# Gating two row groups a step, early fetches tied to their own scatters, zeros kept in the rows' memory, and a new order of steps

## The chip, the cores and the metric

The kernel runs on one core of one Trainium2 chip. The metric is the device time of one execution in microseconds (us); lower is better. Every number below comes from the profile of the kernel before, from its timed runs, or from the two programs as they are built.

## What is computed

Eight sequences of 1856 rows of 256 values pass a spectral filter, and every filtered row then goes to one of 16 experts. Cut to what matters:

```python
X = np.fft.rfft(x, axis=1)                       # x: (8, 1856, 256)
Yr = Xr @ w_r - Xi @ w_i + b_r
Yi = Xr @ w_i + Xi @ w_r + b_i
Yr, Yi = soft_threshold(Yr, 0.01), soft_threshold(Yi, 0.01)
y = np.fft.irfft(Yr + 1j * Yi, n=1856, axis=1)   # 14848 rows of 256
g = argmax(y @ w_group)                          # 4 groups, gate = softmax value
e = argmax(y @ w_expert[g])                      # 4 experts a group, gate likewise
out = gate_g * gate_e * (relu(y @ w1[g, e]) @ w2[g, e])   # 256 -> 1024 -> 256
```

## The kernel before, in words

The sequences are taken in four pairs. For a pair TensorE runs the forward transform in two stages (`first_a`, L342, into `bank`; `f_mm`, L668, into `pg`), mixes real and imaginary parts with the weights (`m_part`, L723, into `pw`), and runs the inverse transform in two stages (`b_mm`, L771; `p_mm`, L790). Float32 operands are split into a rounded high part, cast on ScalarE, and a low rest, made on VectorE; so `xh` and `xl`, `wh` and `wl`. `m_both` (L723, step k) needs the high part of the sum of both parts, `s_high` (L703, step t, on ScalarE), and a bias that ScalarE writes into `pw` first (`m_bias`, L716, step j). `m_min` (L752 and L754, step o, VectorE) ends the mix; the last `o` of a pair opens its inverse transform (step r).

The rows that come out are turned (`p_turn`, L812), copied to `yt` (L816 on ScalarE, or VectorE), and multiplied with the gate weights (`g_mm`, L831, step G); VectorE turns the logits (`g_turn`, L841, step H), and the route steps (R, L210 to L280) choose the expert and the slot of each row. GpSimd then scatters the rows to the lists of their experts in DRAM, `xs_d` (L293, step S), 128 scatters in all, 32 for a pair, with two to four under way at a time. While the last pair is still routed, eight early jobs already work on the first 256-row pieces of four experts' lists: `e_fetch` (L472 and L477, step F, on SP's queue), `e_turn` (L481, T), `e_high` and `e_low` (L892, L896), `up_mm` (L907, U) and `down_mm` (L928, D). Behind all scatters come the remaining jobs (L520 onward), whose code is the same in both kernels.

Lists that are not full must hold zeros. `clear_steps` (step Z) writes them from a block of zeros with 17 transfers that ScalarE issues (L434 once, 130 KB; L436 sixteen times, 1170 KB each).

The order on TensorE, ScalarE, VectorE and SP is written out: a string `ORDER` of 1884 letters, one letter a step, is walked from the left, and each engine gets the instructions of its steps in that order. GpSimd's order is left to the scheduler. The loads and the first transform of pair 0 stand ahead of the string, in an order of their own; on SP they are the eight pieces of `x` for pair 0 (`big`), then weights, bias and tables, then four pieces of 1024 KB of pair 1's `x` into `v` (L355), then `CI` and `wg`.

Transfers of SP and of ScalarE share eight completion semaphores (`DMAHW0` to `DMAHW7` in the rows of order below), taken in turn in the order of the program. A transfer that takes one again is issued only when the transfer that had it before has landed; the engine that is to issue it waits in its own stream of instructions.

Of the kernel before, what the change touches and what calls it, by code (L numbers as in the profile page):

```python
# [10 lines left out]
F32 = mybir.dt.float32  # L11
# [10 lines left out]
K1 = 15  # L22
# [43 lines left out]
ejefgfhitgeukhijqeptukmoqfgmhicotupjmkfoqmoghepijtefguhkmimqootcjpukdqmfZgmoehiptojfZguemkhcqmoiotjpfZukgdqehi  # L66
mmoptojfZugcmmdkhqoeitopujkmfZgomqheitpclojufZgdmkehoqmitojpfZgukmmedqhplitfZgouojmmchocioktjeqpumfZgddokmqhci
otpjumedfZogmkqehitojpukmoqefZmogpjhitemmukofZogjhrqpitsumekmsfZrgohioqstjusepfZkqgmohripmfZssmotoeghriusjekts
mocjcqdupfZkdcqmgvdompcwlohjmifmtducexdgkohyqcivdopwGHlmcvemfjtoguwhiotkxquypjefkmdomgchvoiqtduGpjwxmkmfgqhyix
ltpoHGeoHjmumkoyfgoqhivtGpHRjeuwRRfkRmglqRxeomhioRpvtjfyRukmRRRqRgehmRRiptGRRomoRHfomujRvegRokhwRqxiRjtuwRpRfk  # L70
gRmxqRmhioopytjRuGmmyRHkqefoopgRhiemtjumGfkooRqgrhjiptuekRHfmegsRsmohiRrSqotussjpkmfmqvogowjpxheityukrqfGmgRom
phsHesmfoRitjouRgrkhieqstRmepsSmSoucRRjSSRvkwRdSRfcgSRxqRhmpyivdSocRtofgGuhRwcSmdljRRiHRdRRkqxomyecSStcRpRRoRd
dRufGljvghcwkHiRxmmqoRpeSytdojRRfScgRmvuhoRmwkqeiRtdlupojfGHSvRkqxmmwRRogpeyoShmSxiGtomvSufghjHRRkiqoteRRRSSRy
pjSuRkvRRmfqGoghwSpmioRteRjuRkRSSHfmxqoSpRghmRoyeRiRSwGtSmjvfwSSRRRRRuSgHkRqhiRxRtmoxRSoRpSyjeuRRkGRfqghimomyp
mmeoRHotoGHuRRfRjSghitrkujeqsRRspRmfkgomRqhrRopssmeSjRfiotRgumrhRitkSReqloRpSusRjfkesmgRRmoqhriotRSjRpuRmSskfW
# [98 lines left out]
def spectral_moe(ctx: ExitStack, tc: tile.TileContext, x, wri, bri, wgate, w1, w2, cst, out):  # L174
# [1219 lines left out]
```

## Time and profile before

| | |
|---|---|
| median of 3 runs | 1055.45 us (1054.57 to 1057.11) |
| the profiled execution | 1054.6 us, span 1052.8 us |
| mean granted TensorE clock | 0.993 |
| TensorE busy | 1016.0 us, 97% of the span |
| VectorE, ScalarE, GpSimd busy | 67%, 52%, 24% |

The profile shows one execution. An engine's row gives the start, the duration, the line, what is written and read, and in brackets how long the engine sat idle before it and which instruction or transfer ended that. A row may merge several instructions, with the count behind "x". The granted clock is 1.00 at 2.4 GHz and 0.50 at 1.2 GHz.

The stages can be read off lines: the first `f_mm` is at 17 us, the last `o` of the four pairs ends at 80.6, 161, 247.6 and 329.15 us, and the remaining jobs begin at 466.07 us.

### The profile page before, as it was taken

The page shows a single profiled execution, that of the slowest core. Times are in us where ns is not written, and L with a number is a line of the kernel's source. Part 1 is how long each engine was busy: PE and PEld are TensorE (multiplying, and loading weights), DVE is VectorE, ACT ScalarE, POOL GpSimd, SP SyncE. Part 2 cuts the span into 40 slices and gives each one's busy share as a digit, 9 for nine tenths or more (in the row PEclk, how much of TensorE's full clock was granted, in tenths as well). Part 3 has the DMA queues.
Part 4 walks back from the last instruction along what each step waited for, and adds up shares of the span by engine and source line. Part 5 has one row for each costly group of instructions (what it writes and reads, how often), then busy time and mean ns, then how long its engine had stood idle before and what let it go on. Part 6 is the DMA issues. An engine that isn't in the chain of part 4 may idle for free.

```text
span 1052.8 us, 20013 instructions
## 1 busy us (share of the span) xinstructions
PE 1016.0 (97%) x7078; PEld 857.9 (81%) x7078; DVE 704.4 (67%) x1764; ACT 549.6 (52%) x1428; POOL 255.1 (24%) x262
## 2 busy tenths in 40 slices
PE   7999999999996999999999999999999999999996
PEld 4886787677874678998899999988889899999995
DVE  6889678988987477647677656475465566566551
ACT  2664685575873464434554535455354455455442
POOL 1000003245355517641121211212211121212111
PEclk9999999999998999999999999999999999999998
DMA  9776401421132156565343232431431431432100
GB/s 379 289 308 239 162 1 38 158 87 69 51 103 81 65 140 185 171 204 148 113 138 112 59 109 53 145 115 49 136 111 51 138 107 52 146 113 63 33 26 25
DMA packets 110065, 125.62 MB, mean 119 GB/s; under 512 B 86250, under 2 KB 86923, under 8 KB 105098
## 3 DMA queue, kind: packets, MB, share of 16 engines
q1 hardware_dynamic: 91386, 74.31, 24.1%
q0 software_dynamic: 11888, 30.67, 7.8%
q10 hardware_dynamic: 6688, 19.34, 4.7%
q8 instruction: 57, 0.93, 0.4%
q14 instruction: 46, 0.38, 0.1%
HBM read 74.32 MB, written 51.75 MB: 120 GB/s over the span
## 4 chain that ended last, share of the span: by engine, by line
PE 79%; issue 6%; DVE 5%; DMA 4%; ACT 3%; POOL 2%; SPq 1%; POOLq 0%; ACTq 0%; DVEq 0%
PE ph L520 26%; PE py L592 16%; PE pw L723 11%; PE py L593 8%; PE pg L668 4%; PE ph L907 3%; DMA xs_d<-v,sloti 2%; PE bank L771 2%; PE bank L342 2%; PE bank L790 2%; PE bank L812 1%; PE py L611 1%; POOL xs_d L293 1%; PE pg L831 1%; PE pg L928 1%
## 5 line engine op out<-in xcount | busy, mean ns | idle before, releaser
L592 PE MATMUL py<-big,hh 128*128 128x512 f32 (+2 forms) x792 | 275.9, 393 | 0.1
L520 PE MATMUL ph<-xth,big 128*128 128x384 f32 (+14 forms) x1024 | 274.3, 346 | 1.6 <-DVE hl L528 0.8
L578 POOL DMA_INDIRECT out_dram<-yo,si x120 | 122.3, 1019 | 484.8 <-DVE si L315 234.0
L528 DVE SCALAR_TENSOR_TENSOR hl<-ph,hh 128x256 fp32r<-128x256 f32 x472 | 157.5, 372 | 98.4 <-ACT hh L524 71.6
L593 PE MATMUL py<-big,hl 128*128 128x256 f32 (+2 forms) x792 | 221.0, 279 | 0.0
L524 ACT ACTIVATE hh<-ph 128x256 fp32r<-128x256 f32 x472 | 140.2, 345 | 113.3 <-PE ph L520 112.6
L520 PEld LDWEIGHTS ph<-xth,big 128*128 128x128 f32 x1024 | 185.4, 188 | 13.6 <-ACT xth L506 1.9
L293 POOL DMA_INDIRECT xs_d<-v,sloti x128 | 126.2, 986 | 284.0 <-DVE big L754 147.8
L520 PE MATMUL ph<-xtl,big 128*128 128x384 f32 (+14 forms) x512 | 176.8, 345 | 1.2 <-DVE xtl L507 1.2
L592 PEld LDWEIGHTS py<-big,hh 128*128 128x128 f32 (+2 forms) x792 | 147.4, 186 | 34.6 <-issue 1.2
L593 PEld LDWEIGHTS py<-big,hl 128*128 128x128 f32 (+2 forms) x792 | 148.0, 187 | 0.3
L600 DVE SCALAR_TENSOR_TENSOR yo<-py,si,yo 128x256 f32<-128x256 f32 (+2 forms) x99 | 47.7, 482 | 108.9 <-ACT yo L599 108.9
L599 ACT ACTIVATE yo<-py,si 128x256 f32<-128x256 f32 (+2 forms) x99 | 46.8, 473 | 131.4 <-PE py L593 121.4
L520 PEld LDWEIGHTS ph<-xtl,big 128*128 128x128 f32 x512 | 96.3, 188 | 7.0 <-DVE xtl L507 2.3
L723 PE MATMUL pw<-wh,xh 128*128 128x256 f32 x360 | 81.3, 308 | 1.6 <-DVE pw L733 1.1
L745 ACT ACTIVATE th<-pw,CF 128x256 f32<-128x256 f32 x120 | 61.1, 526 | 36.8 <-PE pw L723 23.5
L723 PEld LDWEIGHTS pw<-wh,xh 128*128 128x128 f32 x360 | 54.3, 189 | 29.0 <-DVE pw L733 9.4
L723 PE MATMUL pw<-wh,xl 128*128 128x256 f32 x360 | 71.4, 280 | 0.9 <-DVE xl L707 0.9
L723 PE MATMUL pw<-wl,xh 128*128 128x256 f32 x360 | 71.0, 279 | 0.0
L668 PEld LDWEIGHTS pg<-CF,big 128*128 128x128 f32 x480 | 58.4, 191 | 12.6 <-issue 3.1
L668 PE MATMUL pg<-CF,big 128*128 128x128 f32 x480 | 64.6, 278 | 4.2 <-DVE xs L698 2.1
L723 PEld LDWEIGHTS pw<-wh,xl 128*128 128x128 f32 x360 | 54.9, 189 | 1.1 <-DVE xl L707 1.1
(187 smaller groups left out, 1557.4 us busy)
## 6 DMA issues: line engine op xcount, KB each, us to landing
xt<-in_w_dram SPq DMA_DIRECT2D x22, 1024.0 KB, 6.1
xs_d<-zero ACTq DMA_DIRECT2D x16, 1170.0 KB, 5.0
whole<-in_w_dram SPq DMA_DIRECT2D x16, 1024.0 KB, 8.1
xt<-in_x_dram SPq DMA_DIRECT2D x8, 1024.0 KB, 5.4
xg<-xs_d SPq DMA_DIRECT2D x48, 96.0 KB, 2.3
big<-in_x_dram SPq DMA_DIRECT2D x8, 512.0 KB, 4.9
v<-in_x_dram SPq DMA_DIRECT2D x4, 1024.0 KB, 14.1
xg<-xs_d SPq DMA_DIRECT2D x24, 128.0 KB, 3.2
```

Of the source, the lines that this page charges most:

```text
L293: ins = nc.gpsimd.indirect_dma_start(out=xs_d, out_offset=bass.IndirectOffsetOnAxis(ap=sl_, axis=0), in_=row, in_offset=None, bounds_check ...
L520: nc.tensor.matmul(o[:, :w], lhsT=a_[:, ch, fs], rhs=b_[:, ch, 0:w], start=k == 0, stop=k == 5)
L524: nc.scalar.activation(out=hh[:, f, :m], in_=ov, func=AF.Relu)
L528: nc.vector.scalar_tensor_tensor(out=hl[:, f, :m], in0=ov, scalar=0.0, in1=hh[:, f, :m].bitcast(F32), op0=ALU.max, op1=ALU.subtract)
L578: ins = nc.gpsimd.indirect_dma_start(out=out, out_offset=bass.IndirectOffsetOnAxis(ap=ids.si[0:m, t:t + 1], axis=0), in_=ysb, in_offset=No ...
L592: nc.tensor.matmul(o, lhsT=hh[:, f, ts], rhs=w2b[:, :, f, :], start=f == 0, stop=f == 7, skip_group_check=True)
L593: nc.tensor.matmul(o[:, 0:D], lhsT=hl[:, f, ts], rhs=w2h[:, f, :], start=False, stop=f == 7, skip_group_check=True)
L599: nc.scalar.activation(out=ysb, in_=o[:, D:], func=AF.Copy, scale=gate_w)
L600: nc.vector.scalar_tensor_tensor(out=ysb, in0=o[:, 0:D], scalar=gate_w, in1=ysb, op0=ALU.mult, op1=ALU.add)
L668: nc.tensor.matmul(f_view(pr, k)[:, ch, :, bt], lhsT=zys[pr][:, k, bt, ch * 128:(ch + 1) * 128], rhs=T_v[:, k, :], start=True, stop=True)
L723: nc.tensor.matmul(y[:, half * D:(half + 1) * D], lhsT=a_[:, ch, t], rhs=w_[:, t, ch], start=False, stop=True, skip_group_check=True)
L745: nc.scalar.activation(out=units["t", pr, k][:, ri], in_=psum["m", pr, k][:, ri * D:(ri + 1) * D], func=AF.Relu, bias=nlam, scale=sg_col(0 ...
```

## The change

- Start: the weights `w_r`, `w_i` are loaded between the second and the third piece of `x`, and the first piece of the table is shorter. The last piece of `x` is fetched and transformed in two halves. Eight more warm-up matmuls stand behind the second `first_a`. GpSimd makes the difference and the sum of the weights, and ScalarE casts them, ahead of the first `f_mm`. The whole start is under the written order.
- Gate: `g_mm` and `g_turn` take two row groups a step: 16 steps in place of 32, with the same 512 matmuls but 16 transposes of 128x256 in place of 32 of 128x128; `yt` has two buffers.
- `psum` of `f_mm` is given back by whichever of two VectorE reads comes last.
- `e_fetch`: a fetch of an early job waits for the last scatters of its own rows, not for later ones.
- The zeros live in the first three rows of `v`, which the first `b_turn` (step s) overwrites; so all Z steps are now ahead of it.
- Pools of the early jobs take their waits by tile.
- `ORDER`: 1852 letters, searched anew. The first Z is letter 7 (72 before), the sixteenth is letter 250 (340 before); the first F and T stand directly behind the last o.

```diff
 ORDER = """
-ejefgfhitgeukhijqeptukmoqfgmhicotupjmkfoqmoghepijtefguhkmimqootcjpukdqmfZgmoehiptojfZguemkhcqmoiotjpfZukgdqehi
+eejfgihZtegiuftkZheZqpgiujkmqfcmotZohupgjkedqifmmhopetgoujmikoqlcmftohgjuipkmqfmephooZtgejmZudfkitqlomojhZucpg
...
+    for c in range(8):
+        if c == 2:
+            nc.sync.dma_start(out=wraw[:, 0:2].rearrange("p a c e -> p (a c e)"), in_=wri)
+        if c == 7:
+            nc.sync.dma_start(out=CF[:, 0:one], in_=cst[:, 0:one])
+            for h in (0, 512):
+                nc.sync.dma_start(out=flat[0][:, c, h:h + 512], in_=flat[1][:, c, h:h + 512])
+        else:
+            nc.sync.dma_start(out=flat[0][:, c], in_=flat[1][:, c])
+    nc.sync.dma_start(out=bias.rearrange("p a e -> p (a e)"), in_=bri)
+    nc.sync.dma_start(out=CF[:, one:three], in_=cst[:, one:three])
+    nc.sync.dma_start(out=craw, in_=cst[:, CF1:CI0])
+    nc.sync.dma_start(out=CF[:, three:], in_=cst[:, three:CF1])
+    nc.sync.dma_start(out=K, in_=cst[:, CK0:CK1])
+    for c in range(0, 8, 2):
+        nc.sync.dma_start(out=xbig[1][:, c:c + 2], in_=x_v[1, :, c:c + 2])
...
+    nc.scalar.copy(out=wh[:, 2], in_=w_r)
+    nc.gpsimd.tensor_tensor(out=dif, in0=w_i, in1=w_r, op=ALU.subtract)
+    nc.scalar.copy(out=wh[:, 0], in_=dif)
+    nc.gpsimd.tensor_tensor(out=tot, in0=w_i, in1=w_r, op=ALU.add)
+    nc.scalar.copy(out=whs, in_=tot)
+    nc.scalar.activation(out=wh[:, 1], in_=tot, func=AF.Copy, scale=-1.0)
...
-    zero = cf.tile([128, 3, RW], F32, name="zero")
+    zero = vv[:, 0, 0:3]
     nc.gpsimd.memset(zero, 0.0)
...
-        yts[pr, u] = wi.tile([128, 2, 4, 128], F32, name="yt", bufs=1)
+        yts[pr, u] = wi.tile([128, 2, 4, 128], F32, name="yt", bufs=2)
...
-    @steps_of(pairs, u8)
+    @steps_of(pairs, range(0, 8, 2))
     def g_mm(pr, u):
         psum["g", pr, u] = pg.tile([128, 512], F32, name="pg")
-        o, yt = psum["g", pr, u], yts.pop((pr, u))
-        for ch in range(2):
-            for q in range(4):
-                nc.tensor.matmul(o[32 * q:32 * q + 32, 0:128], lhsT=wg[:, ch], rhs=yt[:, ch, :, 32 * q:32 * q + 32],
-                                 start=ch == 0, stop=ch == 1)
+        o = psum["g", pr, u][:, 0:256].rearrange("p (h v z) -> p v h z", h=2, v=2)
+        for v in range(2):
+            yt = yts.pop((pr, u + v)).rearrange("p c (h x) t -> p c h x t", h=2)
+            for ch in range(2):
+                for q in range(4):
+                    nc.tensor.matmul(o[32 * q:32 * q + 32, v], lhsT=wg[:, ch], rhs=yt[:, ch, :, :, 32 * q:32 * q + 32],
+                                     start=ch == 0, stop=ch == 1)
...
         for ins in reads:
             tc.add_to_no_dep_group("early rows", ins.ins)
+            for k in range(64 + 32 * j, len(sent)):
+                tc.declare_no_dep(ins.ins, group=f"row{k + 1}", reason="later rows go to slots behind those of the early jobs")
+            for k in range(64 + 32 * j - FLY[1 + j], 64 + 32 * j):
+                tc.add_manual_dep(ins.ins, sent[k], landed, reason="the early job's rows have landed")
```

The order of ScalarE at the start, before: rows of the first two mix steps (`wh` is a weight, `xh` and `xim` come from `f_mm`, `th` from the mix), with the semaphores that each waits for; the zeros (L434, L436) stand 33 rows from the start.

```order
L680 CAST xh<-pg 128x2x256 [waits PE_49]
L685 COPY xim<-pg 128x256
L408 CAST wh<-xt 128x512 [waits DVE_49] x2
L680 CAST xh<-pg 128x2x256 [waits PE_49]
L703 CAST xh<-xs 128x2x128 [waits DVE_49]
L685 COPY xim<-pg 128x256 [waits Activation_49]
L716 ACTIVATE pw<-bias,CF 128x256
```

The same place now (L692 and L697 are L680 and L685 of before, L724 is L703, L737 is L716, L447 and L449 are L434 and L436).

```order
L692 CAST xh<-pg 128x2x256 [waits PE_49]
L697 COPY xim<-pg 128x256
L447 DMA xs_d<-v 128x260 [waits DMAHW1_49]
L449 DMA xs_d<-v 384x1x780 [waits DMAHW2_49]
L724 CAST xh<-xs 128x2x128 [waits DVE_49]
L697 COPY xim<-pg 128x256 [waits PE_49,Activation_49]
L701 CAST sl<-th 128x128 [waits DMAHW6_49]
L692 CAST xh<-pg 128x2x256 [waits DVE_49]
L724 CAST xh<-xs 128x2x128
L449 DMA xs_d<-v 384x1x780 [waits DMAHW3_49]
L449 DMA xs_d<-v 384x1x780 [waits DMAHW4_49]
L697 COPY xim<-pg 128x256 [waits PE_49,Activation_49]
L737 ACTIVATE pw<-bias,CF 128x256
```

Four transfers of zeros moved ahead of the second `m_bias` (L737 in the last row), two of them ahead of the first `s_high`. The order of SP at the same place now, the last four loads of `x` for pair 1 with the semaphores they take over:

```order
L374 DMA v<-in_x_dram 128x2x1024 [waits DMAHW1_49]
L374 DMA v<-in_x_dram 128x2x1024 [waits DMAHW2_49]
L374 DMA v<-in_x_dram 128x2x1024 [waits DMAHW3_49]
L374 DMA v<-in_x_dram 128x2x1024 [waits DMAHW4_49]
L436 DMA CI<-in_cst_dram 128x192 [waits DMAHW5_49]
```

A transfer waits for the semaphore that it takes itself, so these four hold `DMAHW1` to `DMAHW4`, the four that the first four transfers of zeros wait for on ScalarE. In the program as it is built each of those four waits for the value that the matching load of `v` brings.

The order of TensorE behind the last mix of pair 3, before (`bank<-big,CI` is the inverse transform, step r; `pg<-oh` belongs to the route steps; `ph` is the first early job):

```order
L771 MATMUL bank<-big,CI 64x512 x16
L261 MATMUL pg<-oh,sl 128x256
L263 MATMUL pg<-oh,ones 128x256
L907 MATMUL ph<-xth,big 128x256
L907 MATMUL ph<-xtl,big 128x256
```

And now:

```order
L792 MATMUL bank<-big,CI 64x512 x8
L260 MATMUL pg<-oh,sl 128x256
L262 MATMUL pg<-oh,ones 128x256
L934 MATMUL ph<-xth,big 128x256
L934 MATMUL ph<-xtl,big 128x256
```

Half of the inverse transform's first stage moved behind the early job's first matmuls. SP's first early fetch, which waited for the last `o` and for the landing of a scatter of the third pair, now waits for the last `o` and for scatters of the first two pairs alone.

## Rows read from the trace of the kernel before

**Rows 1.** Windows: stretch, then busy us (instructions) by engine, granted clock, DMA, GB/s.

```profile
core 0: us, PE busy (x) PEld busy (x) DVE busy (x) ACT busy (x) POOL busy (x), PEclk, DMA share, GB/s
17.00:85.40 68.40, 65.03 (x524) 54.66 (x524) 56.21 (x112) 44.45 (x103) 2.56 (x3) 1.00 0.78 311
85.40:172.00 86.60, 85.88 (x791) 64.73 (x790) 69.53 (x147) 54.43 (x126) 1.98 (x2) 1.00 0.29 105
172.00:260.00 88.00, 85.66 (x812) 63.73 (x808) 73.31 (x179) 55.00 (x129) 36.41 (x38) 1.00 0.29 100
260.00:329.16 69.16, 64.23 (x622) 51.66 (x626) 60.09 (x162) 52.19 (x121) 34.02 (x35) 1.00 0.22 78
329.16:466.07 136.91, 126.45 (x972) 101.72 (x964) 85.89 (x198) 60.70 (x118) 68.99 (x71) 0.96 0.47 138
```

**Rows 2.** Timeline of TensorE, 17 to 27 us: start, duration, instruction, idle before.

```profile
17.01 1.83 PE L668 MATMUL pg<-CF,big 128*128 128x128 f32 x14 [1.48 <-DVE big L372]
20.04 1.13 PE L668 MATMUL pg<-CF,big 128*128 128x128 f32 x8 [1.20 <-DVE xs L698]
22.27 0.50 PE L723 MATMUL pw<-wh,xl 128*128 128x256 f32 x2 [0.86 <-DVE xl L707]
...
26.54 0.66 PE L342 MATMUL bank<-v,cA 64*64 64x512 f32 x4
```

**Rows 3.** Timeline of ScalarE, 14 to 24 us.

```profile
18.46 0.38 ACT L685 COPY xim<-pg 128x256 f32<-128x256 f32 x1
18.73 1.15 ACT L408 CAST wh<-xt 128x512 fp32r<-128x512 f32 x2
...
20.24 0.43 ACT L703 CAST xh<-xs 128x256 fp32r<-128x256 f32 x1
...
20.81 0.51 ACT L716 ACTIVATE pw<-bias,CF 128x256 f32<-128x256 f32 x1
```

**Rows 4.** Waits of SP's queue: us in total, times, longest.

```profile
SPq L644 <- DMA xs_d<-zero: 45.3, 1, 45.3
```

**Rows 5.** Timeline of SP, 0 to 36 us, and DMA issues of the page.

```profile
12.01 3.44 SPq L355 DMA_DIRECT2D v<-in_x_dram  x4
...
v<-in_x_dram SPq DMA_DIRECT2D x4, 1024.0 KB, 14.1
```

**Rows 6.** Windows, 20 to 29 us, and the issues of zeros (min/median/max ns).

```profile
20.00:29.00 9.00, 7.71 (x60) 6.41 (x60) 5.73 (x11) 4.14 (x11) 1.94 (x2) 1.00 1.03 417
...
xs_d<-zero ACTq DMA_DIRECT2D x16, 1170.0 KB, 5.0
...
xs_d<-zero ACTq DMA_DIRECT2D x1, 130.0 KB
...
L436 ACTq DMA_DIRECT2D xs_d<-zero x16: 541/542/630, 37.3 to 102.3; - x16
```

**Rows 7.** Waits of TensorE, 24 to 329.16 us.

```profile
PE pg L831 <- ACT yt L816: 2.7, 2, 2.4
```

**Rows 8.** Lines L841 and L816 by form: min/median/max ns.

```profile
L841 DVE STREAM_TRANSPOSE L<-pg x32: 273/307/317, 115.2 to 399.7; 128x128 f32<-128x128 f32 x32
...
L816 ACT COPY yt<-bank x32: 992/1014/1081, 110.4 to 396.3; 128x1024 f32<-128x1024 f32 x32
```

**Rows 9.** Timeline of TensorE, 328 to 339.4 us.

```profile
328.69 1.95 PE L771 MATMUL bank<-big,CI 64*64 64x512 f32 x16 [1.54 <-DVE big L752]
332.19 4.06 PE L771 MATMUL bank<-big,CI 64*64 64x512 f32 x16 [1.55 <-DVE v L780]
339.27 0.37 PE L261 MATMUL pg<-oh,sl 128*128 128x256 bf16 x1 [3.02 <-DVE oh L255]
```

**Rows 10.** Windows around the fall and the return of the clock.

```profile
334.00:335.00 1.00, 1.00 (x6) 0.24 (x2) 0.00 (x0) 0.00 (x0) 0.85 (x1) 0.56 0.43 122
...
345.00:346.00 1.00, 1.00 (x13) 0.45 (x16) 1.00 (x3) 0.60 (x1) 0.07 (x1) 1.00 0.00 0
```

**Rows 11.** Timelines of VectorE, SP and GpSimd, 328 to 374 us.

```profile
328.68 0.47 DVE L754 SCALAR_TENSOR_TENSOR big<-pw,CF,th 128x256 f32<-128x256 f32 x1
...
333.70 0.38 SPq L472 DMA_DIRECT2D xi<-xs_d  x1
...
338.01 0.71 DVE L481 STREAM_TRANSPOSE sl<-xg 128x512 f32<-128x512 f32 x1 [4.46 <-DMA xg<-xs_d]
...
344.92 0.23 DVE L280 TENSOR_SCALAR sloti<-slot,K 128x16 int32<-128x16 f32 x1
...
370.59 0.97 POOL L293 DMA_INDIRECT xs_d<-v,sloti  x1 [0.40 <-DMA xs_d<-v,sloti]
372.99 0.39 SPq L472 DMA_DIRECT2D xi<-xs_d  x1
```

More of the change, by code (lines that the diff above doesn't have):

```diff
@@ L71 @@
[L71 to L75, printed above, removed]
@@ L377, in drain @@
             pass
-    o = pg.tile([128, 512], F32, name="pg")
+    warm = pg.tile([128, 512], F32, name="pg")
     for _ in range(14):
-        nc.tensor.matmul(o[:, 0:256], lhsT=ones, rhs=smask[16], start=True, stop=True)
+        nc.tensor.matmul(warm[:, 0:256], lhsT=ones, rhs=smask[16], start=True, stop=True)
     for _ in range(2):
@@ L387, in spectral_moe @@
+    for i in range(7):
         o = bank()
         first_a(0, i, o)
-        a_last = turn_a(0, i, o)
-    craw = wf.tile([128, 2 * D], F32, name="th")[:, 0:128]
-    wraw = xp.tile([128, 4, 2, D], F32, name="xt")
-    nc.sync.dma_start(out=wraw[:, 0:2].rearrange("p a c e -> p (a c e)"), in_=wri)
-    nc.sync.dma_start(out=craw, in_=cst[:, CF1:CI0])
-    bias = cf.tile([128, 2, D], F32, name="bias")
-    nc.sync.dma_start(out=bias.rearrange("p a e -> p (a e)"), in_=bri)
-    nc.sync.dma_start(out=CF[:, first:], in_=cst[:, first:CF1])
@@ L411, in spectral_moe @@
-    mix_parts(2, 0)
-    nc.scalar.copy(out=sl, in_=craw)
-    nc.vector.tensor_tensor(out=bias[:, 0], in0=bias[:, 0], in1=bias[:, 1], op=ALU.subtract)
-    behind.close()
-    nc.vector.memset(nlam, -2 * LAM)
+        turn_a(0, i, o)
+        if i == 1:
+            for _ in range(8):
+                nc.tensor.matmul(warm[:, 0:256], lhsT=ones, rhs=smask[16], start=True, stop=True)
+    for h in range(2):
+        last_half(h)
     T_v = CF[:, CF1 - K1 * 128:CF1].rearrange("p (k m) -> p k m", m=128)
-    late = ExitStack()
@@ L427, in spectral_moe @@
     nc.sync.dma_start(out=wgp, in_=wgate)
-    late.close()
-    zero = cf.tile([128, 3, RW], F32, name="zero")
+    zero = vv[:, 0, 0:3]
     nc.gpsimd.memset(zero, 0.0)
+    cf.tile([128, 16], F32, name="behind")
     def clear_steps():
@@ L685, in f_im, with f_read @@
         nc.scalar.copy(out=xi, in_=f_part(pr, k)[:, :, 1])
-        if pr == k == 0:
-            mix_parts(0, 2)
-            mix_parts(1, 3)
+        if (pr, k) == (0, 0):
+            nc.vector.tensor_tensor(out=bias[:, 0], in0=bias[:, 0], in1=bias[:, 1], op=ALU.subtract)
+        if (pr, k) == (0, 1):
+            nc.scalar.copy(out=sl, in_=craw)
+    read = set()
+    def f_read(pr, k):
+        if (pr, k) in read:
+            del psum["f", pr, k]
+        read.add((pr, k))
     @steps_of(pairs, k15)
@@ L839, in g_turn @@
             logits[pr, u // 4] = rt.tile([128, 16, 32], F32, name="L")
[L840 to L841 removed]
+        L = logits[pr, u // 4].rearrange("p (h i) m -> p h i m", h=2)[:, :, 2 * (u % 4):2 * (u % 4) + 4]
+        nc.vector.transpose(out=L, in_=psum.pop(("g", pr, u))[:, 0:256].rearrange("p (h i m) -> p h i m", h=2, i=4))
     def route_steps():
```

106 lines of the change are left out of this document (55 added, 51 removed).

## The prediction

> **What bounds the kernel now.** I read the page first: TensorE is busy 97% of the span, so I ask where the missing part lies and which wait ends last there. The windows by stage [rows 1] say it: between 85.40 and 172 us 0.7 us of 86.6 are missing, up to 260 us 2.3, up to 329.16 us 4.9, and from there to the first remaining job 10.5. From 466.07 us the code of both kernels is the same, so whatever the change does it does ahead of that point, and a loss or gain there reaches the end one to one. Then I read four places: the start on TensorE and ScalarE [rows 2, 3], the transfers [rows 4 to 6], the gate's waits [rows 7, 8], and the end of the last pair [rows 9 to 11].
>
> At the start the first transform of pair 0 feeds TensorE at 17.01 us, small waits on VectorE follow, and at 26.54 us it begins the transform of pair 1, whose first operand is in `v` [rows 2]. The order up to that instruction has the same steps in both kernels, so 26.54 us is the mark that I carry to the changed kernel.
>
> **The zeros move into the start: +8.1 us.** This is the term with the most weight. In the new order ScalarE meets four transfers of zeros between the first `xim` and the second `m_bias`. Each takes a semaphore that one of the four loads of `v` holds, so ScalarE stands still until that load has landed. That an engine is held by a transfer of the other queue is no theory: SP's load at L644 waited 45.3 us for a transfer of zeros [rows 4]. The four loads are issued from 12.01 us over 3.44 us, the last some 0.37 us before the end of that, at 15.1 us, and need 14.1 us to land [rows 5]; the last piece is thus there at 29.2 us. In the kernel before the first large transfer of zeros is issued only at 37.3 us [rows 6], when nothing of this is on its way, so the trace of before shows no such wait on ScalarE.
>
> What is queued behind it: the first `s_high`, which the first mix needs, behind the first two; one `xim` and the second `m_bias`, which the second mix needs, behind all four. TensorE goes through the first mix and then waits. From the landing of the last piece to the transform of pair 1 there is the issue of the transfer, 0.54 us [rows 6], a copy of 0.38 and a bias of 0.51 [rows 3], and six matmuls of the second mix, some 0.8 us by the 0.50 us for two, which overlap [rows 2]: 2.2 us. With the landing at 29.2 us the mark moves to 31.4 us, a loss of 4.9 us. That is the lower bound of the term, if ScalarE is held at all.
>
> The zeros also carry bytes. From 20 to 29 us the DMA engines are full, share 1.03, at 417 GB/s with SP's loads alone [rows 6]. The first two transfers of zeros go out when the first two pieces of `v` have landed, ahead of the last piece: 130 and 1170 KB [rows 6]. If they take their part of the same engines, the last piece comes later by 1.33 MB at 417 GB/s, 3.2 us. If they found room beside it, by nothing. The row with its share of 1.03 is nearest, and it leaves no room: I take 3.2 and get 4.9 + 3.2 = 8.1 us. The Trainium skill, in "DMA: Bandwidth & Descriptors", section "Issuing engines are not separate DMA queues", speaks against this change: transfers that ScalarE, SP and GpSimd start run on the same 16 engines and interleave. By it the term is 8.1, by free room it would be 4.9; no run here shows both queues at once.
>
> Two more costs bound it from above. The third transfer of zeros, 1170 KB, goes out at the third piece's landing and may take its 2.9 us from the last piece too. And the granted clock may fall. At 334 us it stood at 0.56, near the level of 1.2 GHz, after TensorE had stood still three times within some 7 us, and at 345 us it was back at 1.00 [rows 10]; sixteen matmuls of the same form that took 1.95 us at the full clock took 4.06 there [rows 9], 2.1 us more. A stall of 5 us or so at the start may bring that. In the kernel before the clock stayed at 1.00 through the idle stretches of the start [rows 1, 2], so I leave it out of the sum. Upper bound: 8.1 + 2.9 + 2.1 = 13.1 us.
>
> **The rest of the start: 0.** The casts of the weights, 1.15 us on ScalarE [rows 3], leave the stretch between `xim` and `s_high`. That would let the first mix start up to 1.15 us sooner; but it now waits for the landings, which are the cover. Without that wait it is a gain of 1.15. The last piece of `x` in halves shortens the last transpose, but the weights' 512 KB go ahead of it; bounds -1 and +1 from the 1.48 us that TensorE waited for that transpose [rows 2], taken as 0. Eight warm-up matmuls lie where TensorE waits for `x`: 0.
>
> **Gates by twos: -2.0 us.** The matmuls stay 512. On TensorE up to the end of the last mix 2.7 us are waits of the gate for the copy to `yt`, 2.4 of them in one place [rows 7]; two buffers and half as many meetings can take away all of it, or, where the second copy of 1.01 us [rows 8] now holds up both groups, cost one such copy. Bounds -2.7 and +1.0; I take -2.0, near the one large wait. The transposes on VectorE fall from 32 of 0.307 us, 9.8 us, to 16, between 16 of 0.307, 4.9 us, and 16 of 0.71, a transpose of 128x512 [rows 11], 11.4 us; beside TensorE, so 0.
>
> **Early fetch: -2.5 us.** Before, the first fetch leaves SP at 333.70 us, 4.5 us after the last `o` ends at 329.15 [rows 11]; now it may leave directly behind that `o`. The turn at 338.01 us ended an idle time of 4.46 us of VectorE, and TensorE stood still 3.02 us before 339.27 [rows 9, 11]. All of the early job's first part can thus come 4.5 us sooner. What it is worth is bounded by the next fetch: that one waits for the scatters that follow the slots of 344.92 us, the last of them at 370.59, and leaves at 372.99 us [rows 11]; GpSimd sets that pace, and the half of the inverse transform that the slots wait for is not sooner. Late next is therefore that fetch. Bounds 0 and -4.5; I take -2.5, a little above the middle since sooner work also spares a part of the half clock at 334 us.
>
> **The new order elsewhere: -3.0 us.** Between 85.40 and 329.16 us TensorE misses 0.7 + 2.3 + 4.9 = 8.0 us [rows 1], 2.7 of them counted above. 5.3 are left to a better order. A worse one can cost as much as the worst of these windows loses now, 4.9. I take -3.0, somewhat over half of what is there, since [rows 1] show most of it in one window.
>
> **Room and psum: 0.** The zeros in the rows' memory only force Z ahead of the first inverse stores, which is priced above; 17 transfers are 17 issues of 0.54 us on ScalarE in both kernels. psum given back by the later of two reads, and pools that wait by tile, change waits that the rows of before do not name: 0.
>
> **Sum.** +8.1 - 2.0 - 2.5 - 3.0 = +0.6 us on the profiled execution of 1054.6 us: 1055.2. That execution lies 0.85 us under the median of 1055.45, so I forecast 1056.0 us on the median's scale. A measurement of this kernel tells about 0.2%, 2.1 us, from no change; this is no change.
>
> **The rivals.**
>
> *Faster: ScalarE is hardly held at the start.* If the loads of `v` land as before, the zeros find room and the loss stays at 4.9, while gate, fetch and order reach -2.7, -4.5 and -5.3: -7.6 us, 1048 us. If the waits are already met when ScalarE comes to them, the start even gains its 1.15. For it: the sequence of steps is the old one and three stages have idle time to give. Against: the semaphores in the built program and the 14.1 us of [rows 5].
>
> *Slower: the zeros hold the start for longer.* One mechanism: transfers of zeros wait for loads that the zeros themselves slow down, and TensorE, idle meanwhile, drops to the lower clock. At its upper bound, 13.1 us, with the gains as I took them, -7.5, it is +5.6: 1061 us. It decides against the change from the point at which the last piece of `v` lands later than some 34 us: 29.2 + 3.2 there cost 8.1, and 1.5 us more make 9.6, which is the 7.5 of gains and the 2.1 of a measurement. For it: the DMA share of 1.03 [rows 6] and the fall of the clock at 334 us [rows 10]. Against: the clock of 1.00 through the start before.
>
> *The change does not do what it says.* The fetch leaves sooner, but the chain of slots and scatters sets the same end, and the new order gives nothing: 8.1 - 2.0 = +6.1, 1061.5 us. For it: the pace of GpSimd [rows 11].
>
> **How the numbers follow.** Forecast 0.40, of which 0.28 within 0.2% and 0.06 on each side; faster rival 0.28; slower rival 0.25; no gain behind the start 0.07. Faster 0.06 + 0.28 = 0.34, same 0.28, slower 0.06 + 0.25 + 0.07 = 0.38. Both signs hold most of the chance: the forecast alone lies between 1053 and 1059 us. For 8 in 10 the range goes from the faster rival, 1048, to 2 us beyond the slower one, where some of the gains are missing too: 1063.
>
> **What would show it.** Right: ScalarE idle in the first 35 us behind an issue of zeros, ended by the landing of `v`; the first matmul on `v` near 34.6 us; a first early fetch within 1 us of the last `o`; fewer waits of the gate on `yt`. Wrong: the first matmul on `v` before 28 us, which takes the largest term away; or the remaining jobs beginning more than 3 us sooner or later than 466 us plus 0.6.

## The result, and the profile after

The changed kernel is slower: 1067.37 us, the median of 4 runs (1064.35 to 1069.72), beside 1056.12 us before (4 runs). The ratio is 1.0103, with a 95% interval from 1.0079 to 1.0126. The forecast was no change at 1056.0 us with a range up to 1063.0; the time lies above the range. The profiled execution is the slowest of the four, 1069.72 us with a span of 1067.9, so the difference of the two profiled executions, 15.1 us, comes out 3.9 us larger than that of the medians, 11.25.

Windows of the changed kernel: busy time by engine, granted clock, DMA share and GB/s, as in [rows 1].

```profile
17.00:42.00 25.00, 18.72 (x125) 15.40 (x124) 12.25 (x27) 9.53 (x24) 0.00 (x0) 0.86 1.03 410
...
95.00:180.00 85.00, 80.40 (x721) 60.94 (x718) 61.54 (x130) 52.10 (x121) 0.00 (x0) 1.00 0.15 51
180.00:260.00 80.00, 78.09 (x754) 59.17 (x757) 68.51 (x162) 51.70 (x121) 31.63 (x32) 1.00 0.29 101
260.00:340.00 80.00, 74.46 (x734) 60.28 (x724) 71.02 (x185) 58.02 (x134) 35.93 (x37) 1.00 0.20 70
340.00:480.00 140.00, 123.19 (x963) 102.49 (x964) 84.40 (x188) 60.12 (x117) 74.52 (x76) 0.91 0.45 132
```

TensorE misses 6.3 us of the first 25, which is the start; 4.6, 1.9 and 5.5 us in the three windows up to the last `o`; and 16.8 us of the 140 behind it, where [rows 1] show 10.5 of 136.9. Measured by marks, the first matmul on `v` is 6.6 us later than before (33.13 and 26.54), the way from there to the last `o` 4.6 us longer (307.2 and 302.6), and the way from the last `o` to the first remaining job 4.7 us longer (140.9 and 136.2; that job's first matmul stands at 465.30 us before, and the 466.07 of the stages named ahead is its second row). So the time went at two ends and in the middle. There the waits of the mix for VectorE and ScalarE grew: 7.2 us of TensorE's time from 42 us to the last `o`, beside 1.4 before. The two ends look like this.

The start, on ScalarE (timeline; L692, L697, L724 and L737 are L680, L685, L703 and L716 of before; ACTq is its issue of a transfer), against [rows 3]:

```profile
19.29 0.38 ACT L697 COPY xim<-pg 128x256 f32<-128x256 f32 x1
22.12 0.36 ACTq L447 DMA_DIRECT2D xs_d<-v  x1
24.58 0.63 ACTq L449 DMA_DIRECT2D xs_d<-v  x1
25.25 0.41 ACT L724 CAST xh<-xs 128x256 fp32r<-128x256 f32 x1 [5.58 <-DMA v<-in_x_dram]
...
27.39 3.76 ACTq L449 DMA_DIRECT2D xs_d<-v  x2
31.25 0.37 ACT L697 COPY xim<-pg 128x256 f32<-128x256 f32 x1 [3.94 <-DMA v<-in_x_dram]
31.51 0.48 ACT L737 ACTIVATE pw<-bias,CF 128x256 f32<-128x256 f32 x1
```

Four transfers of zeros go out one by one at 22.1, 24.6, 27.4 and 30.6 us, and the two idle stretches of ScalarE, 5.58 and 3.94 us, end with a landing of `v`. On TensorE (timeline), against [rows 2], with the windows of the granted clock behind:

```profile
25.71 0.79 PE L744 MATMUL pw<-wh,xh 128*128 128x256 f32 x2 [3.71 <-ACT xh L724]
...
27.79 2.07 PE L680 MATMUL pg<-CF,big 128*128 128x128 f32 x8
...
32.05 0.50 PE L744 MATMUL pw<-wh,xh 128*128 128x256 f32 x2 [0.34 <-ACT pw L737]
...
33.13 1.09 PE L341 MATMUL bank<-v,cA 64*64 64x512 f32 x8
...
20.00:25.00 5.00, 1.13 (x8) 0.97 (x8) 0.81 (x3) 0.00 (x0) 0.00 (x0) 0.89 1.03 420
25.00:30.00 5.00, 4.02 (x16) 3.65 (x17) 1.94 (x4) 1.76 (x5) 0.00 (x0) 0.50 1.03 401
30.00:35.00 5.00, 4.66 (x33) 3.40 (x32) 2.52 (x7) 3.13 (x8) 0.00 (x0) 0.93 1.03 416
```

The first matmul on `v` is at 33.13 us in place of 26.54, 6.6 us later. TensorE's long wait lay ahead of the first mix, and the clock then stood at 0.50, the level of 1.2 GHz: eight matmuls of `f_mm` took 2.07 us where eight of the same form took 1.13 at 20.04 in [rows 2]. Ahead of the second mix, at 32.05 us, TensorE stood still for only 0.34 us: its slowed work and ScalarE's wait for the last landing ended almost together.

The other end is behind the last `o`, which ends at 340.32 us (timelines of VectorE, SP, TensorE and GpSimd), against [rows 9, 11]:

```profile
339.85 0.47 DVE L775 SCALAR_TENSOR_TENSOR big<-pw,CF,th 128x256 f32<-128x256 f32 x1
...
340.46 0.38 SPq L485 DMA_DIRECT2D xi<-xs_d  x1
...
348.07 0.37 PE L260 MATMUL pg<-oh,sl 128*128 128x256 bf16 x1 [5.62 <-DVE oh L254]
...
357.64 0.23 DVE L279 TENSOR_SCALAR sloti<-slot,K 128x16 int32<-128x16 f32 x1
...
388.05 0.97 POOL L292 DMA_INDIRECT xs_d<-v,sloti  x1 [0.30 <-issue]
...
390.46 0.39 SPq L485 DMA_DIRECT2D xi<-xs_d  x1
...
397.13 0.58 PE L934 MATMUL ph<-xth,big 128*128 128x256 f32 x1 [10.16 <-ACT xth L919]
```

The first early fetch leaves 0.1 us behind the last `o`, as it should; before it was 4.5. But the second one leaves 50.1 us behind it, where [rows 11] give 372.99 - 329.15 = 43.8 us, and TensorE then stands still for 10.16 us. It also stands still for 5.62 us ahead of the route step at 348.07, beside 3.02 in [rows 9]. Behind the last `o` the granted clock falls twice, to 0.53 from 341 to 352 us and to 0.51 from 389 to 403 us; before it fell once, from 334 to 345 [rows 10]. Between the last `o` and that fetch GpSimd sends 27 scatters; before it was 22.

### The profile page after: what moved, and what is told of

Same layout as the page of the kernel before. It is cut to its first block, busy times and chain, and to the rows that moved or that the text cites. A ratio compares the mean times of both kernels' runs of the same rounds, so it can differ in the third digit from the quotient of the medians.

```text
span 1067.9 us, 20029 instructions
## 1 busy us (share of the span) xinstructions
PE 1018.4 (95%) x7094; PEld 864.5 (81%) x7094; DVE 700.7 (66%) x1747; ACT 549.9 (51%) x1429; POOL 258.2 (24%) x264
## 4 chain that ended last, share of the span: by engine, by line
PE 76%; DVE 8%; ACT 4%; DMA 4%; issue 4%; POOL 1%; SPq 0%; ACTq 0%; POOLq 0%; DVEq 0%
PE ph L533 25%; PE py L605 15%; PE pw L744 8%; PE py L606 8%; PE ph L934 5%; PE pg L955 3%; PE pg L680 2%; PE bank L341 2%; PE bank L792 2%; PE bank L833 2%; DMA v<-in_x_dram 1%; PE pg L956 1%; PE py L624 1%; PE bank L811 1%; DVE v L801 1%
## 5 line engine op out<-in xcount | busy, mean ns | idle before, releaser
L533 PEld LDWEIGHTS ph<-xth,big 128*128 128x128 f32 x1024 | 185.3, 188 | 13.1 <-ACT xth L519 1.3
L680 PE MATMUL pg<-CF,big 128*128 128x128 f32 x480 | 65.5, 280 | 2.3 <-DVE base L446 1.2
L680 PEld LDWEIGHTS pg<-CF,big 128*128 128x128 f32 x480 | 59.3, 193 | 8.5 <-issue 3.4
L934 PE MATMUL ph<-xth,big 128*128 128x256 f32 x256 | 52.8, 296 | 10.2 <-ACT xth L919 10.2
## 6 DMA issues: line engine op xcount, KB each, us to landing
v<-in_x_dram SPq DMA_DIRECT2D x4, 1024.0 KB, 15.1
```

The source lines that it names most:

```text
L533: nc.tensor.matmul(o[:, :w], lhsT=a_[:, ch, fs], rhs=b_[:, ch, 0:w], start=k == 0, stop=k == 5)
L680: nc.tensor.matmul(f_view(pr, k)[:, ch, :, bt], lhsT=zys[pr][:, k, bt, ch * 128:(ch + 1) * 128], rhs=T_v[:, k, :], start=True, stop=True)
L934: nc.tensor.matmul(o[:, i * 256:(i + 1) * 256], lhsT=a_[:, ch, fs], rhs=b_[:, ch, :], start=k == 0, stop=k == 5)
```

## The experiments

All kernels ran beside runs of the kernel before on the same chip, and but for e11 to e16 the kernel before stood between 1055.0 and 1056.1 us. Times are medians; where a difference of two experiments is named, it is that of their medians, and the interval given is that of each one's ratio to the kernel before.

**Are the zeros what holds the start? e1 moves them back, e2 moves them up in the kernel before.** The edit in e1 is four letters of `ORDER`, which go from the places 7, 16, 19 and 34 to 96, 149, 179 and 231 (counted from 0); in e2 it is the first four Z of the order of before, which go to 7, 16, 19 and 34. The first Z issues two transfers, so the four letters are five transfers, one more than the expectations say.

```diff
-eejfgihZtegiuftkZheZqpgiujkmqfcmotZohupgjkedqifmmhopetgoujmikoqlcmftohgjuipkmqfmephooZtgejmZ...
+eejfgihtegiuftkheqpgiujkmqfcmotohupgjkedqifmmhopetgoujmikoqlcmftohgjuipkmqfmephooZtgejmZ...
```

> The changed kernel with its first four transfers of zeros moved behind the 96th, 149th, 179th and 231st step of the order, all still ahead of the first inverse store; nothing else differs. Theory (ScalarE is held by the landings of v): ScalarE issues no zeros in the first 35 us, the first matmul on v comes at 26.5 to 27.5 us in place of 33.1, the clock stays at 1.00 there, and the time falls by 6 to 7 us to about 1061. What is left against the kernel before, 4 to 6 us, then sits behind that mark. Rival (the start is slow for another reason, the weights' load ahead of x or the last piece in halves): the mark stays beyond 30 us and the time near 1067.

> The kernel before with its first four transfers of zeros moved up to the letters where the changed kernel has them; nothing else differs. Theory: ScalarE is held here too, but its four transfers take over the semaphores of K and of the first three loads of v, one load earlier than in the changed kernel, so the first matmul on v moves from 26.5 to between 29 and 31 us and the time rises by 3 to 5 us to 1059 to 1061. Rival: the mark stays at 26.5 us and the time at 1055 to 1056.

Measured: e1 1068.52 us, ratio 1.0108 (1.0085 to 1.0132), no faster than the changed kernel. Its first matmul on `v` is at 25.44 us, so both theory and rival of the expectation are half wrong: the start came back whole, and the time did not. Where it went (e1, VectorE and TensorE, and windows around it; L801 is the first inverse store, L792 what TensorE does behind it):

```profile
90.00 1.25 DVE L801 STREAM_TRANSPOSE v<-bank 128x1024 f32<-128x1024 f32 x1 [7.62 <-DMA xs_d<-v]
...
91.31 5.14 PE L792 MATMUL bank<-big,CI 64*64 64x512 f32 x16 [5.83 <-DVE v L801]
...
53.40:80.00 26.60, 26.35 (x212) 22.05 (x211) 22.49 (x47) 17.55 (x41) 0.00 (x0) 1.00 1.03 394
80.00:91.00 11.00, 5.48 (x46) 3.79 (x45) 3.12 (x6) 2.03 (x5) 0.00 (x0) 0.98 0.64 245
91.00:97.00 6.00, 5.70 (x19) 1.91 (x20) 5.37 (x10) 2.19 (x5) 0.00 (x0) 0.50 0.00 0
```

The zeros live where the first inverse store writes, so that store waits until all 17 transfers have been read out. In e1 the DMA engines run full from 53 to 80 us (share 1.03), and still the last transfer comes 7.62 us late; the granted clock falls behind that stall, to 0.50 from 91 to 97 us. In the changed kernel the same store waits 0.90 us: there the price is paid at the start instead. The zeros' place sets a date, and the bytes ahead of it fill the queue.

e2 gave 1061.96 us, ratio 1.0062 (1.0039 to 1.0085): 6.6 us above the kernel before beside it, 1055.39. The first matmul on `v` came at 29.50 us, as expected; the time is 1 us above the expected range, since ScalarE was held again at the fifth transfer, by a landing of `CI`, so that the time lost more than the mark (e2, ScalarE):

```profile
27.91 0.40 ACT L703 CAST xh<-xs 128x256 fp32r<-128x256 f32 x1 [5.54 <-DMA v<-in_x_dram]
...
35.02 0.48 ACT L716 ACTIVATE pw<-bias,CF 128x256 f32<-128x256 f32 x1 [3.55 <-DMA CI<-in_cst_dram]
```

This is the mechanism of the forecast, shown by itself, with the zeros in memory of their own: an early transfer holds ScalarE until a landing that has nothing to do with zeros.

**Is it the order or the code? e3 and e4 swap them.** e3 is the changed kernel with the order of before (every second G and H kept, four Z moved ahead of the first inverse store). e4 is the kernel before with the new order, each G and H written twice, zeros in `v`, two buffers of `yt`.

> The changed kernel with the order of before: of its 32 G and 32 H every second one is kept, and the four Z that stood behind the first inverse store are moved ahead of it; start, gates by twos, fetch and zeros are those of the change. Theory (the new order is what costs behind the start): 1051 to 1056 us, at or below the kernel before. Rival (gates by twos or the new waits of the fetch cost it): 1060 us or more.

> The kernel before with the changed kernel's order and the zeros where e1_zeros_later has them: each G and each H of it is written twice, so that gates stay one row group a step; yt has two buffers, the zeros live in v, and psum of f_mm is given back by the later read, as that order needs; start and waits of the fetch are those of before. Theory (the order costs): 1060 to 1062 us, as e1_zeros_later. Rival: 1055 to 1056 us.

Measured: e3 1064.04 us, ratio 1.0085 (1.0055 to 1.0115); e4 1091.78 us, 1.0327 (1.0303 to 1.0351). Neither is a clean swap. e3 came out where its rival had it, at 1060 us or more, but not for the rival's reason: it ran into the same date. VectorE stood 11.31 us in front of the first inverse store, which waits for the zeros, and TensorE 9.89 us at 94 us.

```profile
92.55 1.25 DVE L801 STREAM_TRANSPOSE v<-bank 128x1024 f32<-128x1024 f32 x1 [11.31 <-issue]
```

e4 pays for the doubled letters, since the second G of a pair waits until VectorE has turned the first (TensorE's waits: us in total, times, longest):

```profile
PE pg L839 <- DVE L L849: 17.2, 11, 7.9
```

That is not all of the 23 us that e4 lies above e1. e4 tells nothing of the order alone. e3 told what to do next: give the zeros memory of their own.

**Zeros in their own row: e5 to e8.** All four have

```diff
-    zero = vv[:, 0, 0:3]
+    zero = cf.tile([128, RW], F32, name="zero")
...
-            nc.scalar.dma_start(out=xs_d[e * CAP:e * CAP + NZ].rearrange("(p a j) w -> p a (j w)", p=128, j=3),
-                                in_=zero.rearrange("p j w -> p (j w)").unsqueeze(1).broadcast_to([128, NZ // 384, 3 * RW]))
+            nc.scalar.dma_start(out=xs_d[e * CAP:e * CAP + NZ].rearrange("(p a) w -> p a w", p=128),
+                                in_=zero.unsqueeze(1).broadcast_to([128, NZ // 128, RW]))
```

and the Z at the letters of the kernel before. With the row read in smaller pieces the DMA engines have a share of 1.00 in e5 from 26.5 to 80 us, and of 0.76 before, for the same 298 GB/s; so the form of the transfers differs too, though TensorE is busy 52.6 of these 53.5 us in both. e5 keeps the new order, e6 has the old one, e7 is e6 with `g_mm` and `g_turn` of before, e8 is e6 without the loops over `sent` in `e_fetch`.

> The changed kernel with the zeros in a row of their own again (one row, read three times as often) and its transfers of zeros at the letters where the kernel before has them; order of all else, gates by twos, start and fetch as changed. Theory (the zeros in the rows' memory force 18.7 MB of zeros through before the first inverse store, and cost 6 to 8 us either at the start or at that store; the new order costs the rest): first matmul on v at 25.5 us, no wait at the first inverse store near 85 us, last o at 332 to 334 us, 1059 to 1061 us. Rival (the zeros' place costs nothing by itself): 1066 us or more.

> As e5_own_zeros_new_order, with the order of before (every second G and H kept, Z where it was). Theory: the start gains 1 us, the fetch 3 to 4 us behind the last o, gates 0 to 2: 1049 to 1052 us, faster than the kernel before. Rival (the code of the change costs by itself): 1055 us or more.

> As e6_own_zeros_old_order, with gates one row group a step as before (32 steps; yt keeps two buffers). If gates by twos are worth the 2.0 us of the prediction: 1051 to 1054 us, 2 us above e6. If they are worth nothing: as e6 within 1 us; the wait of the gate for yt of 2.4 us near 322 us decides, it is there in one and not in the other.

> As e6_own_zeros_old_order, without the new waits of the early fetch: a fetch waits again for scatters of later rows. If the fetch's waits are worth the 2.5 us of the prediction or the 3.9 us that e3_old_order_new_code gained behind the last o: the first fetch leaves 4 to 5 us behind the last o, and the time is 2.5 to 4 us above e6. Rival (GpSimd's pace sets the next fetch anyway): as e6 within 1 us.

| | median us | ratio to before (interval) | first matmul on `v` | last `o` ends | second fetch behind it | first remaining job |
|---|---|---|---|---|---|---|
| before, profiled | 1054.6 | | 26.54 | 329.15 | 43.8 | 465.30 |
| changed, profiled | 1069.7 | | 33.13 | 340.32 | 50.1 | 481.21 |
| e5 | 1061.61 | 1.0053 (1.0035 to 1.0071) | 25.78 | 334.15 | 49.4 | 473.02 |
| e6 | 1054.23 | 0.9975 (0.9960 to 0.9989) | 26.21 | 332.81 | 41.4 | 465.99 |
| e7 | 1052.27 | 0.9956 (0.9933 to 0.9978) | 25.52 | 331.04 | 40.0 | 460.62 |
| e8 | 1055.26 | 1.0001 (0.9988 to 1.0014) | 25.69 | 330.91 | 43.0 | 464.60 |

The columns behind the ratio are from the profiled execution of each. What follows:

- The zeros' place: changed kernel 1067.37 to e5 1061.61 us, 5.8 us. e5 starts at 25.78 us and has no wait at the first inverse store, as expected; the time is 0.6 us above the expected range. Taken against the kernel before beside each, the difference is 4.8 us.
- The new order: e6 to e5, 7.4 us, with intervals far apart. The larger part lies behind the last `o`: from there to the first remaining job it is 138.9 us in e5 and 133.2 in e6, and the second fetch is 8.0 us later.
- e6 itself misses its expectation of 1049 to 1052 us: it is 0.9 us below the kernel before beside it, 1055.14.
- Gates by twos: e7 to e6, 2.0 us slower, with the sign opposite to the forecast; the two intervals still overlap, so this is likely rather than shown. The profiled execution of e6 is the slowest of its ten and that of e7 the fastest of its five, so their columns, 5.4 us apart at the first remaining job, overstate it.
- The fetch's waits: e8 to e6, 1.0 us gained; the first fetch leaves 0.1 us behind the last `o` in e6 and 3.4 in e8. The intervals touch, and 1.0 us is what the rival allowed, not the 2.5 to 4 of the theory.

On the gates the waits of TensorE up to the last `o` say more than the medians (e6, gates by twos, then e7, one at a time; us in total, times, longest):

```profile
PE pg L854 <- ACT yt L837: 2.5, 1, 2.5
PE pw L744 <- DVE pw L754: 2.1, 4, 1.0
PE pw L744 <- ACT pw L737: 1.2, 4, 0.6
PE pw L744 <- DVE xl L728: 0.9, 1, 0.9
```

```profile
PE pg L853 <- ACT yt L838: 2.7, 2, 2.5
PE pw L745 <- DVE pw L755: 1.1, 3, 0.5
PE pw L745 <- ACT pw L738: 0.2, 1, 0.2
```

The wait of the gate for `yt`, the one that I meant to save, is there in both, so two buffers and fewer meetings did not take it away; in the changed kernel, with its new order, TensorE has no such wait up to the last `o`. What grew by twos are the waits of the mix for VectorE and ScalarE, 4.2 us in place of 1.3.

**Why is the second fetch late in the new order? e9 and e10 let GpSimd keep four scatters of the third pair under way.**

```diff
-FLY = (2, 2, 2, 4)
+FLY = (2, 2, 4, 4)
```

> As e5_own_zeros_new_order, with four scatters of the third pair under way in place of two. In e5 the slots of that pair's second half stood 16.6 us behind the last o, 27 scatters came between the last o and the second early fetch, 1.74 us apart, and TensorE stood still 9.2 us for that fetch. Theory (in the new order the route steps of that pair come later, and GpSimd's pace then sets the fetch): the slots stay near 16.6 us, the scatters come 1.3 to 1.5 us apart, the fetch leaves 40 to 43 us behind the last o in place of 49.4, and the time falls by 5 to 8 us to 1054 to 1057. Rival (the fetch or TensorE waits for something else, such as the early weights): time within 2 us of 1061.6.

> As e7_e6_single_gates, with four scatters of the third pair under way in place of two. There the fetch left 40.0 us behind the last o and TensorE waited 1.3 us near it. Theory: it leaves 34 to 37 us behind the last o, but TensorE has work until then, so the time falls by no more than 3 us, to 1049 to 1052. Rival (the pace of the scatters sets the end of the early jobs too): 1045 to 1048.

Measured: e9 1052.29 us, ratio 0.9976 (0.9964 to 0.9989), 9.3 us below e5 and below the range expected; e10 1047.60 us, 0.9930 (0.9913 to 0.9947), 4.7 below e7. The slots of the third pair's second half, SP's second fetch and TensorE's waits at the route step and for that fetch in e5 (new order, two scatters), e6 (old order, two) and e9 (new order, four):

```profile
340.80 0.37 PE L260 MATMUL pg<-oh,sl 128*128 128x256 bf16 x1 [5.02 <-DVE oh L254]
...
350.74 0.24 DVE L279 TENSOR_SCALAR sloti<-slot,K 128x16 int32<-128x16 f32 x1
...
383.52 0.39 SPq L485 DMA_DIRECT2D xi<-xs_d  x1
...
389.30 0.58 PE L934 MATMUL ph<-xth,big 128*128 128x256 f32 x1 [9.21 <-ACT xth L919]
```

```profile
344.68 0.23 DVE L279 TENSOR_SCALAR sloti<-slot,K 128x16 int32<-128x16 f32 x1
...
345.69 0.97 POOL L292 DMA_INDIRECT xs_d<-v,sloti  x1 [5.85 <-DVE hl L944]
...
374.19 0.39 SPq L485 DMA_DIRECT2D xi<-xs_d  x1
...
379.95 0.58 PE L934 MATMUL ph<-xth,big 128*128 128x256 f32 x1 [3.55 <-ACT xth L919]
```

```profile
340.57 0.28 PE L260 MATMUL pg<-oh,sl 128*128 128x256 bf16 x1 [4.04 <-DVE oh L254]
...
351.50 0.97 POOL L292 DMA_INDIRECT xs_d<-v,sloti  x1 [4.09 <-issue]
...
373.66 0.39 SPq L485 DMA_DIRECT2D xi<-xs_d  x1
...
380.88 0.39 PE L934 MATMUL ph<-xth,big 128*128 128x256 f32 x1 [1.02 <-ACT xth L919]
```

From e5 to e9 the slots stay where they were, 16.6 and 16.8 us behind the last `o`; only the scatters come closer, and the fetch leaves 40.0 us behind it in place of 49.4. GpSimd, which in e5 begins the sixteen scatters of the second half 4.9 us after their slots stand, now stands still 4.09 us ahead of them. So two scatters at a time could not carry what the order leaves behind the last `o`: 27 scatters in e5, 20 in e6.

That is not the whole cost of the order. Its slots also come later than those of the old order, 16.6 us behind the last `o` in e5 against 11.9 in e6, and TensorE stands still for 5.02 us ahead of the route step, where e6 shows no such wait: around the last `o` one block of 16 matmuls of the inverse transform stands ahead of that step in e5, and two in e6. Four scatters change neither; e9 still waits 4.04 us there. And the pace helps the old order too: e10 gains 4.7 us by it, more than the 3 expected and inside the rival's range. So of the 7.4 us the pace explains some 4.6 (9.3 less 4.7). What is left between e9 and e10, 4.7 us, holds the gates by twos, 2.0, and some 2.7 of the order; these splits are estimates from differences of medians.

**The same edit in the two kernels alone: e11 to e18.** e11, e13, e15 and e18 are the changed kernel with that line, e12, e14, e16 and e17 the kernel before with it.

> The changed kernel, with four scatters of the third pair under way in place of two and nothing else. Theory (the zeros' place and the late scatters cost separately): the scatters give back what they gave in e9 against e5, 8 to 9 us, and the zeros' place stays at 5 to 7 us: 1057 to 1060 us, first matmul on v still near 33 us. Rival (the two overlap, so that the stall behind the last o hides the start's delay): 1052 to 1055 us.

> The kernel before, with four scatters of the third pair under way in place of two and nothing else. Its second early fetch left 43.8 us behind the last o, and TensorE had no single wait over 1.6 us near it. Theory (the pace of the scatters is worth much only where the order leaves more of them behind the last o): 1051 to 1054 us, 2 to 4 us below the kernel before. Rival: 1055 us, nothing, or 1047 us, as much as in e9.

> The same kernel as e11_after_four_scatters, the changed kernel with four scatters of the third pair under way, beside a kernel before at its usual 1055 us. Theory (the zeros' place and the late scatters cost separately): 1057 to 1060 us, the second early fetch 40 to 42 us behind the last o in place of 50.1, first matmul on v still near 33 us. Rival (the two overlap): 1052 to 1055 us.

> The same kernel as e12_before_four_scatters, the kernel before with four scatters of the third pair under way, beside a kernel before at its usual 1055 us. Theory (the pace of the scatters is worth much only where the order leaves more of them behind the last o): 1051 to 1054 us. Rival: 1055 us, nothing, or 1047 us, as much as in e9.

> The same kernel as e11 and e13, the changed kernel with four scatters of the third pair under way, once more beside a kernel before that should stand at 1055 us. Theory (the zeros' place and the late scatters cost separately): 1057 to 1060 us, the second early fetch 40 to 42 us behind the last o in place of 50.1, first matmul on v still near 33 us. Rival (the two overlap): 1052 to 1055 us.

> The same kernel as e12 and e14, the kernel before with four scatters of the third pair under way, once more beside a kernel before that should stand at 1055 us. Theory (the pace of the scatters is worth much only where the order leaves more of them behind the last o): 1051 to 1054 us. Rival: 1055 us, nothing, or 1047 us, as much as in e9.

> The same kernel as e12, e14 and e16, the kernel before with four scatters of the third pair under way, a last time. Beside a kernel before at 1055 us: theory (the pace of the scatters is worth much only where the order leaves more of them behind the last o) 1051 to 1054 us; rival 1055 us, nothing, or 1047 us, as much as in e9. Beside a kernel before near 1097 us again: it says nothing of either.

> The same kernel as e11, e13 and e15, the changed kernel with four scatters of the third pair under way, a last time. Beside a kernel before at 1055 us: theory (the zeros' place and the late scatters cost separately) 1057 to 1060 us, the second early fetch 40 to 42 us behind the last o in place of 50.1; rival (the two overlap) 1052 to 1055 us. Beside a kernel before near 1097 us again: it says nothing of either.

Beside e11 to e16 the kernel before itself took 1095 to 1101 us in the median, so these six (1115 to 1130 us, 1.6 to 3.1% above it) are inconclusive. The profiled execution of e13, 2030.73 us, says nothing. The other profiles show engines standing still at several places with nothing that the profile could name behind it, as in e16:

```profile
317.80 0.80 PE L723 MATMUL pw<-wh,xh 128*128 128x256 f32 x2 [6.08 <-issue]
```

Beside e17 and e18 the kernel before took 1055.75 and 1055.04 us. e17, the kernel before with four scatters, took 1051.58 us, ratio 0.9957 (0.9943 to 0.9971): 4.2 us gained, at the lower end of what was expected. e18, the changed kernel with four, took 1058.72 us, 1.0030 (1.0019 to 1.0041), 8.7 below the changed kernel and inside the 1057 to 1060 of the theory; its second fetch leaves 40.1 us behind the last `o`, and its first matmul on `v` is at 33.37 us. The two losses are separate: with four scatters the zeros' place costs 6.4 us (e18 less e9) beside 5.8 with two. But the kernel before gains 4.2 us from the same line, so about half of the 8.7 is not a loss that the change brought.

The best kernel of the study is e10: the start and the fetch of the change, the order and gates of before, zeros in their own row, four scatters; 1047.60 us, 0.7% below the kernel before.

## Why the prediction was wrong, by its own steps

**The zeros move into the start, +8.1 us: right in mechanism, somewhat high.** ScalarE was held by the landings of `v` exactly as read from the order of ScalarE and SP. From the last landing to the mark it was 2.5 us against the 2.2 worked out. The last piece landed at 30.6 us, 1.4 us later than 29.2, where I took 3.2. Its way from issue to landing, in the changed kernel and in e1, which has no zeros before 36 us (issues of the two pages; only the last piece's landing is in the traces), and the bytes of SP's queue (q1) and ScalarE's (q10) in the changed kernel from 22.1 to 30.6 us:

```profile
v<-in_x_dram SPq DMA_DIRECT2D x4, 1024.0 KB, 15.1
...
v<-in_x_dram SPq DMA_DIRECT2D x4, 1024.0 KB, 13.7
...
q1 hardware_dynamic: 1016, 2.98, 88.0%
q10 hardware_dynamic: 255, 0.48, 14.7%
```

So the zeros held the last piece up by 1.4 us. I had let all 1.33 MB of the first two transfers go ahead of it; by then 0.48 MB had moved, which at the 406 GB/s of this stretch is 1.2 us. The first issue was at 22.1 us, and ScalarE's queue moved no packet before 25.5. The clock, which I left out of the sum, did fall, but nearly all of it lay beneath the wait for the landing: TensorE stood still 0.34 us ahead of 32.05. Against e5, where the zeros go late, the mark moved by 7.3 us and the end by 5.8, both inside the bounds of 4.9 and 13.1. The Trainium skill, in "DMA: Bandwidth & Descriptors", section "Issuing engines are not separate DMA queues", says that transfers that different engines start interleave on the same 16 engines. The trace agrees: from 30.6 to 36 us the two queues moved 336 and 335 packets. The row of the clock was also misread: ahead of 334 us TensorE had stood still twice, 1.54 and 1.55 us [rows 9], not three times.

**"Room and psum: 0" failed in part.** I saw that the zeros' new place forces Z ahead of the first inverse store, and took the cost as paid at the start. e1 shows that it isn't the place of four letters: with the start freed the store waited 7.62 us. The cost belongs to the date and the bytes.

**"The new order elsewhere: -3.0 us" is the step that failed.** It measured +7.4 (e6 to e5), outside its own bounds of -5.3 and +4.9. I priced the order by TensorE's idle time ahead of the last `o`, as if the order could only fill or waste that. The larger part came behind it, where I had written that the next fetch is "late next" and that "GpSimd sets that pace", and then bounded the fetch's term at 0, so that nothing in the sum could make that fetch later. The letters would have told a part: ahead of the last `o` stand 76 of the 128 scatter letters before and 73 now; in the trace the slots of the third pair's second half come 17.3 us behind that `o` where [rows 11] give 15.8, and 27 scatters stand between the `o` and the fetch in place of 22. In its place the runs showed three things behind the last `o`: more scatters than two at a time can carry, slots 4.7 us later (e5 and e6), and a wait of TensorE of 5.0 us ahead of the route step. The first is worth some 4.6 us of the 7.4, by e5 to e9 less e7 to e10; the others are read from the traces, and no run takes them out one by one.

**"Gates by twos: -2.0 us" had the sign wrong, as far as the runs tell.** +2.0 (e7 to e6). The row of 2.4 us [rows 7] is a wait for a copy that two buffers did not take away; e6 and e7 both have it, at 2.5 us.

**"Early fetch: -2.5 us" was high but right in kind.** It measured -1.0 (e8 to e6), within 0 and -4.5. The fetch also brings the slots forward, which I had taken as not sooner: 11.9 us behind the last `o` in e6, 14.9 in e8.

**The rest of the start, 0:** without early zeros the mark stood at 25.5 to 26.5 us in the six kernels e5 to e10, 0 to 1 us ahead of 26.54, as bounded.

The sum by what was measured: from the kernel before, 1055.14 us beside e5 to e8, to e7 -2.9, to e6 +2.0, to e5 +7.4, to the changed kernel +5.8, which is 1067.4. The -2.9 holds the start, the fetch, the later giving back of `psum`, the pools and the second buffer of `yt`; only the fetch has a run of its own. The sign for "wrong" came true: the remaining jobs begin at 481 us, 15 later than forecast. Of the rivals the third, 1061.5 us, was nearest: it saw that the chain of slots and scatters sets the end behind the last `o`, but only as a gain that fails to come, and it still lies 6 us short. The slower rival was right that the clock would fall; the last piece landed at 30.6 us, though, well ahead of the 34 it needed, and the start cost less than forecast, not more. None had the order's scatters, slots or the route step's wait as a price.

## What to carry to other kernels

A buffer that lends its memory to constants gets a date: everything that reads them must be through before the first write, and the bytes up to that date have to fit beside what the DMA engines carry already. When an order is searched anew, count for every engine how much work of a limited queue is left behind the last step that feeds it, and test such a limit in the kernel before as well: here it was worth 4.2 us there. And a transfer issued by a computing engine may hold that engine for a landing of another queue, so look up which transfer had its semaphore last.

## What the runs showed that I had not expected

Beside loads that keep the engines full (share 1.03), the zeros' transfers began late: in the changed kernel 3.4 us lie between the first issue, at 22.1 us, and the first packet of ScalarE's queue. The two that went out at 30.6 and 32.1 us took 13.6 and 15.3 us to land, against 4.8 to 5.3 before, while the last load lost only 1.4. And the sixteen scatters of the third pair's second half came 1.70 us apart in e5, with two under way, and 1.31 in e9, with four, although one issue takes 0.97 us in either.
